# Top-k attention into a hardswish feed-forward: quarter-array products for the left-over queries, and another order of the first loads and transposes

## The chip, the core and the metric

The kernel runs on one core of a Trainium2 chip. A core has five engines with their own instruction streams: TensorE (PE, with its weight loads PEld), VectorE (DVE), ScalarE (ACT), GpSimd (POOL) and SyncE (SP). Each engine executes its instructions in the order of its stream and waits for others by semaphores. Sixteen DMA engines move data between HBM and the on-chip memory SBUF; a DMA is issued by an instruction in an engine's stream. TensorE writes its products into PSUM, which has eight banks; a bank holds 512 float32 in each of 128 partitions.

The metric is the device time of one execution in microseconds, as the median of the runs. Lower is better.

## The reference

Two blocks stand one behind the other. The first is attention over 8 batches, 8 heads, 576 positions and a head size of 64, in which each query attends to its 32 best keys alone. The second is a feed-forward block with hardswish over the 4608 rows of 512 that come out.

```python
scores = scale * np.matmul(q, k.transpose(0, 1, 3, 2))          # (8, 8, 576, 576)
kth = np.partition(scores, -32, axis=-1)[..., -32:-31]
scores = np.where(scores >= kth, scores, -1000000000.0)
scores = scores - np.max(scores, axis=-1, keepdims=True)
attn = np.exp(scores)
attn = attn / (np.sum(attn, axis=-1, keepdims=True) + 1e-09)
x = np.matmul(attn, v)                                           # heads joined: (4608, 512)
h = x @ w_in                                                     # (512, 2048), float64 on input
g = h * np.clip(h + 3.0, 0.0, 6.0) / 6.0
out = g @ w_out                                                  # (2048, 512), float64 on input
```

## The kernel before

**Tiles.** The 576 positions of a head are cut into 4 tiles of 128 (J = 4, JP = 512) and a rest of 64 (R). Two heads make a `Pair`: their keys and queries of 64 values each lie side by side, so that 128 rows hold two heads. A `Duo` is two pairs (four heads) with one tile of queries. There are 64 duos with 128 queries and 16 with the 64 left-over queries (`self.rest`), 80 in all.

**One duo.** `scores` (line 200) multiplies the queries with the keys. Each head takes half the rows of TensorE's array (the slices `heads`); the 512 main keys of a head go to one PSUM bank (line 232, for left-over queries line 215), the 64 left-over keys of both heads to the fifth bank (lines 226 and 217). ScalarE copies the banks into the SBUF tile `sc` (lines 233 and 236; 219 and 220 for left-over queries). `top` (line 243) finds the 32 greatest of each row on VectorE: four rounds of MAX8 (line 250, eight greatest values) with MATCH_REPLACE8 (line 254, which strikes them out) between. `shift`, `exp` and `inverse` (lines 259 to 287) turn the rest into weights: GpSimd takes the difference of the 32nd and the first value, ScalarE runs two activations for each row and sums up, VectorE takes the reciprocal. `weights` (line 289) scales on GpSimd and splits the words into halves, `flip` transposes them by a DMA, `join` (line 314) puts them together on ScalarE or GpSimd, and `values` (line 326) multiplies with the values on TensorE.

**The feed-forward block** (line 352) is a generator of pieces for TensorE (lines 365 and 385), ScalarE (373, 375, 395) and GpSimd (379, 380). `piece` issues one after another between the steps of the attention.

**PSUM.** The pool `ps_big` has one buffer of five banks, which the transposes and the scores take in turn through `big()`: the next user waits until ScalarE has copied the last one out. The pool `ps_w` has three buffers of one bank each for the values and the feed-forward block.

**Weights.** The weights come as float64. `convert` (line 96) makes float32 of them in four steps: SP loads a chunk (line 102); ScalarE takes an absolute value and a scaled copy (108, 111) with a clamp by GpSimd between (109); VectorE shifts and joins bits (117, 118); GpSimd adds (123). There are 32 chunks. Each call of `convert_step` moves the pipeline by one: the add of one chunk, VectorE's two instructions of the next, ScalarE's of a later one, and the load of a further one. VectorE's part of a chunk comes two calls after its ScalarE part.

**Order.** The schedule is written out by hand; every engine's stream has the order of the program. Lines 515 to 527 are the prologue: loads of the first pairs, the transpose of pair 0, its scores, the transpose of pair 1, its scores, with three calls of `convert_step` between. Then come slots (line 564), eight for each duo. A slot has one round of `top`, one `convert_step`, and whatever of the other parts is due (the dictionaries `usual`, `behind`, `early` and `soon`). In the first slots the third and the fourth pair are transposed. After the last duo the pieces of the feed-forward block that are left run out.

**A pair's load** (line 146) has six DMAs on SP: the keys of the first head, of the second, the left-over keys of both, and the same for the queries. `transpose` (line 171) turns nine 128x128 tiles through TensorE into the five banks: tiles 0 to 3 are keys, 4 to 7 queries, and tile 8 has the left-over keys and queries. ScalarE copies them out: 1024 columns (line 179), the left-over queries (180), and the left-over keys of each head into `kr` (183), which has zeros elsewhere.

Of the kernel before, what the change touches and what calls it, by code (L numbers as in the profile page):

```python
# [10 lines left out]
F32 = mybir.dt.float32  # L11
# [18 lines left out]
def kernel(  # L30
# [22 lines left out]
    def pool(name, bufs, **kw):  # L53
        return ctx.enter_context(tc.tile_pool(name=name, bufs=bufs, **kw))
# [23 lines left out]
    w_out = const([P, NFC, DM], "w_out")  # L78
# [9 lines left out]
    def big():  # L88

        return ps_big.tile([P, 5 * 512], F32, tag="big", name="big")  # L90
# [48 lines left out]
    class Pair:  # L139
# [3 lines left out]
            self.b, self.hp = b, hp  # L143
            self.vm, self.vr, self.kr = vms[hp], vrs[hp], krs[b % 2 * NHP + hp]

        def load(self):
            h0 = 2 * self.hp
            t = self.landed = kqpool.tile([P, 2 * J + 1, 2, D], F32, tag="kq", name="landed")
            for i, src in enumerate((k, q)):
                for hh in range(2):  # L150
                    nc.sync.dma_start(
                        t[:, i * J : (i + 1) * J, hh, :],
                        src[self.b, h0 + hh, 0:JP, :].rearrange("(p j) d -> p j d", j=J),
                    )
                nc.sync.dma_start(
                    t[i * R : (i + 1) * R, 2 * J, :, :],
                    src[self.b, h0 : h0 + 2, JP:S, :].rearrange("h s d -> s h d"),
                )
# [9 lines left out]
                    self.vr[hh * R : (hh + 1) * R, hh, :], v[self.b, h0 + hh, JP:S, :]  # L168
                )

        def transpose(self):
            kq = kqpool.tile([P, JP + S], F32, tag="kq", name="kq")
            self.kT, self.qT = kq[:, 0:JP], kq[:, JP : JP + S]
            ps = big()
            for j in range(2 * J + 1):
                rows = self.landed[:, j, :, :].rearrange("p h d -> p (h d)")
                nc.tensor.transpose(ps[:, j * P : (j + 1) * P], rows, ident[:])  # L177
            c0 = 2 * JP
            nc.scalar.copy(kq[:, 0:c0], ps[:, 0:c0])
            nc.scalar.copy(kq[:, c0 : c0 + R], ps[:, c0 + R : c0 + 2 * R])  # L180
            for hh in range(2):
                d = slice(hh * D, (hh + 1) * D)
                nc.scalar.copy(self.kr[d, hh, :], ps[d, c0 : c0 + R])

    class Duo:

# [13 lines left out]
        def scores(self, us=(0, 1)):  # L200

            if us[0] == 0:
                self.sc = scpool.tile([P, 2, 2 * (S + R)], F32, tag="sc", name="sc")
                self.den = mpool.tile([P, 2, 2], F32, tag="den", name="den")
            sc, nu = self.sc[:, us[0] : us[-1] + 1, :], len(us)
            ps = big()
            heads = [slice(0, D), slice(D, P)]
            qs = slice(self.qt * P, min(self.qt * P + P, S))
            banks = ps[:, 0 : 4 * 512].rearrange("p (n s) -> p n s", s=512)
            left = ps[:, 4 * 512 :]  # L210
            if self.rest:
# [8 lines left out]
                nc.scalar.copy(  # L220
                    sc[:, :, JP:S], left[:, 0 : nu * R].rearrange("p (u r) -> p u r", r=R)
                )
                return
            for i, u in enumerate(us):
                pr = self.pairs[u]
                nc.tensor.matmul(
                    left[:, i * P : (i + 1) * P], pr.qT[:, qs], pr.kr[:].rearrange("p h r -> p (h r)")
                )
            for i, u in enumerate(us):
                pr = self.pairs[u]  # L230
                for hh, d in enumerate(heads):
                    nc.tensor.matmul(banks[:, 2 * i + hh, :], pr.qT[d, qs], pr.kT[d, :])  # L232
            nc.scalar.copy(  # L233
                sc.rearrange("p u (h s) -> p (u h) s", h=2)[:, :, 0:JP], banks[:, 0 : 2 * nu, :]
            )
            nc.scalar.copy(  # L236
                sc[:, :, JP : JP + P], left[:, 0 : nu * P].rearrange("p (u r) -> p u r", r=P)
            )

        def row(self, u, t):  # L240
            return self.sc[:, u, t * S : (t + 1) * S]
# [174 lines left out]
    per_batch = 2 * J + 2  # L416
    ND = len(duos)
# [4 lines left out]
    left = 0  # L422
# [123 lines left out]
    queued = {}  # L546
    for m in range(ND):
        for part, at in (early if m < 2 else soon if m >= ND - 2 else behind if per_batch <= m < ND - 4 else usual).items():
            queued.setdefault(8 * m + at, []).append((m, part))

    def parts(slot, late=None):
# [12 lines left out]
    for m in range(ND + 3):  # L564
        u = duos[m] if m < ND else None
        for i in range(8):
# [18 lines left out]
            if i == 0:  # L585
                p = pair_at(m, 4)
# [5 lines left out]
            if i == 5:  # L592
                p = pair_at(m, 5)
# [42 lines left out]
```

## Time and profile before

| what | us |
|---|---|
| median of 3 runs (lowest, highest) | 1580.66 (1580.39, 1581.92) |
| the profiled execution's own time | 1580.33 |
| its span, first instruction to last | 1578.5 |
| first MAX8 starts (line 250) | 13.59 |
| last MAX8 ends | 1491.31 |
| MAX8, all: line 250, `m<-wk` and `m<-sc` | 613.1 + 203.3 busy |
| MATCH_REPLACE8, all: line 254, `wk<-m,wk` and `wk<-m,sc` | 423.7 + 211.8 busy |
| conversion on VectorE: lines 117 and 118, 32 of each | 24.8 + 30.2 busy |
| products of left-over queries: lines 215 and 217, 128 of each | 32.8 + 9.0 busy |

Times in the profile are counted from the start of the span. A line of the timeline gives the start, the length, the engine, the program line, the operation with output and input, the number of instructions merged, and in brackets the idle time of the engine before it with what ended that. A line of the waits gives who waited for whom, the total, the number of waits and the longest. One written matmul of float32 stands in the trace as two MATMUL records.

### The profile page before, as it was taken

The numbers are of one execution on the slowest core, as the hardware profiler recorded it, in microseconds if no ns is written. First come the engines' busy times: TensorE is split into PE (matmuls) and PEld (weight loads), VectorE is DVE, ScalarE is ACT, GpSimd is POOL, SyncE is SP. The second block draws the span as 40 slices with busy tenths as digits, with TensorE's granted clock in tenths as the row PEclk, the third lists the DMA queues.
The fourth block names the chain that finished last, engine by engine and source line by source line (L and its number), as shares of the span: only waits on it lengthen the run. The fifth ranks groups of instructions, "written<-read, shape, count | busy, mean of one in ns | idle before, by whom it ended". The sixth has DMA issues, their size and how long they took to land.

```text
span 1578.5 us, 28787 instructions
## 1 busy us (share of the span) xinstructions
PE 1456.9 (92%) x10272; PEld 1039.0 (66%) x10272; DVE 1466.8 (93%) x3105; ACT 1096.3 (69%) x1865; POOL 1144.5 (73%) x1264
## 2 busy tenths in 40 slices
PE   5256799979999999998999999999999999999899
PEld 3153566567767777666777777776777767677675
DVE  6999999999999999999999999999999999999700
ACT  6675777777777777777776786777766787777621
POOL 4868687777867777867687777867687777767841
PEclk9568999989999999999999999999999999999999
DMA  8652543444344543545254543446244443533410
GB/s 236 159 181 45 113 83 81 94 91 97 76 90 89 101 83 76 101 85 119 55 106 76 97 89 82 93 93 116 57 96 87 98 88 74 103 65 68 83 22 14
DMA packets 450319, 144.49 MB, mean 92 GB/s; under 512 B 433280, under 2 KB 441472, under 8 KB 450176
## 3 DMA queue, kind: packets, MB, share of 16 engines
q1 hardware_dynamic: 450176, 142.65, 43.5%
q8 instruction: 81, 1.33, 0.3%
q14 instruction: 62, 0.51, 0.1%
HBM read 45.09 MB, written 9.44 MB: 35 GB/s over the span
## 4 chain that ended last, share of the span: by engine, by line
DVE 51%; PE 35%; POOL 5%; issue 3%; ACT 3%; DMA 1%; SPq 1%; POOLq 0%; ACTq 0%; DVEq 0%
DVE m L250 26%; DVE wk L254 22%; PE h L365 14%; PE acc L385 13%; PE pv L338 4%; PE big L232 3%; POOL e L306 1%; DVE y L118 1%; POOL sc L297 1%; DMA t<-e 1%; POOL eT L318 1%; DVE a L117 1%; PE big L177 1%; ACT sc L278 1%; ACT eT L318 1%
## 5 line engine op out<-in xcount | busy, mean ns | idle before, releaser
L250 DVE MAX8 m<-wk 128x8 f32<-128x576 f32 x864 | 613.1, 746 | 2.2
L385 PE MATMUL acc<-w_out,g 128*128 128x512 f32 x1152 | 516.9, 600 | 14.1 <-POOL g L380 14.1
L365 PE MATMUL h<-xT,w_in 128*128 128x128 f32 x4096 | 485.5, 279 | 17.3 <-ACT xT L348 17.3
L365 PEld LDWEIGHTS h<-xT,w_in 128*128 128x128 f32 x4096 | 475.0, 195 | 39.5 <-issue 18.2
L254 DVE MATCH_REPLACE8 wk<-m,wk 128x576 f32<-128x576 f32 x576 | 423.7, 742 | 0.0
L385 PEld LDWEIGHTS acc<-w_out,g 128*128 128x128 f32 x1152 | 213.6, 191 | 260.4 <-issue 238.6
L297 POOL TENSOR_SCALAR sc<-sc,den 128x576 f32<-128x576 f32 x288 | 213.8, 753 | 229.9 <-DVE den L287 222.7
L306 POOL COPY e<-sc 128x2304 uint16<-128x2304 uint16 (+1 forms) x192 | 320.3, 1678 | 10.2
L278 ACT ACTIVATE sc<-sc,shift 128x576 f32<-128x576 f32 x288 | 220.4, 769 | 40.5 <-POOL shift L266 37.7
L318 ACT COPY eT<-t 128x2304 uint16<-128x2304 uint16 (+1 forms) x82 | 215.9, 2632 | 37.9 <-DMA t<-e 35.3
L273 ACT ACTIVATE sc<-sc,m 128x576 f32<-128x576 f32 x288 | 210.1, 777 | 46.2 <-DVE m L250 46.0
L338 PE MATMUL pv<-eT,vm 128*64 128x128 f32 (+1 forms) x2560 | 164.0, 273 | 57.9 <-ACT eT L318 45.8
L254 DVE MATCH_REPLACE8 wk<-m,sc 128x576 f32<-128x576 f32 x288 | 211.8, 742 | 0.0
L318 POOL COPY eT<-t 128x2304 uint16<-128x2304 uint16 (+1 forms) x78 | 203.8, 2613 | 6.9 <-DMA t<-e 6.5
L338 PEld LDWEIGHTS pv<-eT,vm 128*64 128x64 f32 x2560 | 135.2, 141 | 109.3 <-ACT eT L318 49.7
L250 DVE MAX8 m<-sc 128x8 f32<-128x576 f32 x288 | 203.3, 742 | 2.4 <-ACT sc L236 2.4
L373 ACT ACTIVATE g<-h,three 128x512 f32<-128x512 f32 x144 | 98.5, 684 | 150.0 <-PE h L365 140.6
L380 POOL TENSOR_TENSOR g<-g,hs 128x512 f32<-128x512 f32 x144 | 185.0, 1285 | 12.1 <-POOL g L379 0.2
L233 ACT COPY sc<-big 128x2048 f32<-128x2048 f32 (+1 forms) x65 | 119.3, 1836 | 26.1 <-PE big L232 26.0
L232 PE MATMUL big<-kq 64*128 64x512 f32 x512 | 136.4, 653 | 0.0
L379 POOL TENSOR_SCALAR g<-g 128x512 f32<-128x512 f32 x144 | 89.2, 620 | 62.6 <-ACT g L373 52.4
L395 ACT ACTIVATE o<-acc 128x512 f32<-128x512 f32 x36 | 21.4, 595 | 106.6 <-PE acc L385 106.6
(47 smaller groups left out, 1113.1 us busy)
## 6 DMA issues: line engine op xcount, KB each, us to landing
landed<-in_k_dram SPq DMA_DIRECT2D x64, 128.0 KB, 3.0
landed<-in_q_dram SPq DMA_DIRECT2D x64, 128.0 KB, 3.0
st<-in_moe_w_in_dram SPq DMA_DIRECT2D x16, 512.0 KB, 5.1
vm<-in_v_dram SPq DMA_DIRECT2D x64, 128.0 KB, 2.3
st<-in_moe_w_out_dram SPq DMA_DIRECT2D x16, 512.0 KB, 6.6
out_dram<-o SPq DMA_DIRECT2D x32, 256.0 KB, 2.4
t<-e SPq DMA_TRANSPOSE x160, 4.6
landed<-in_k_dram SPq DMA_DIRECT2D x32, 32.0 KB, 2.8
```

What stands on the lines that cost most here:

```text
L232: nc.tensor.matmul(banks[:, 2 * i + hh, :], pr.qT[d, qs], pr.kT[d, :])
L250: nc.vector.max(self.m[u][:, t, 8 * r : 8 * r + 8], self.cur[t])
L254: nc.vector.match_replace(wk, self.m[u][:, t, 8 * r : 8 * r + 8], self.cur[t], LOWEST)
L273: nc.scalar.activation(row, row, AF.Prelu, bias=m[:, t, TOP_K - 1 : TOP_K], scale=-1.0, alpha=FLAT)
L278: nc.scalar.activation(row, row, AF.Exp, bias=self.less[u][:, t : t + 1], scale=-scale / FLAT, accum_out=self.den[:, u, t : t + 1],)
L297: nc.gpsimd.tensor_scalar(row, row, self.den[:, u, t : t + 1], 1.0, ALU.mult, ALU.mult)
L306: nc.gpsimd.tensor_copy(halves[:, :, to : to + c1 - c0], words)
L318: copy(eT[:, 0 : self.nb, :] .rearrange("p c q -> p (c q)") .bitcast(U16) .rearrange("p (x h) -> p h x", h=2), self.t16[u][:, 0 : 2 * self ...
L338: nc.tensor.matmul(pv[hh * D : (hh + 1) * D, u * w : (u + 1) * w], pr.vm[:, hh, c, :] if c < J else pr.vr[:, hh, :], rhs, start=(c == 0), ...
L365: nc.tensor.matmul(h[:, (f - f0) * P : (f - f0 + 1) * P], w_in[:, i, f * P : (f + 1) * P], xT[:, i, :], start=(i == 0), stop=(i == NHP - 1),)
L380: nc.gpsimd.tensor_tensor(g[:], g[:], hs[:], ALU.mult)
L385: nc.tensor.matmul(acc[:], gs[f // nf][:, f % nf * P : (f % nf + 1) * P], w_out[:, f, :], start=(f == 0), stop=(f == NFC - 1),)
```

## The change

It has four parts.

*Left-over queries.* In `scores` the product of pair `u` and head `hh` goes to the output half `heads[u ^ hh]` in place of `heads[hh]`. With the row half of the head, the four products of a duo then lie in four different quarters of the array. The four main products are issued first, then the four left-over ones, which go to banks 2 and 3. `values` reads the transposed weights at the columns that go with it.

*The first pair's loads.* `load` takes a queue. For the first pair the three query loads are issued by ScalarE.

*The first pair's transpose.* It uses three banks of `ps_w` in place of `big()`: the key tiles; the first query tile with the left-over tile; the other query tiles. ScalarE copies the first two banks as far as the first scores need them, and the remaining queries later, after the first scores. For those first scores the copies into `sc` are split in three: left-over columns, first bank, second bank.

*The prologue.* VectorE fills one chunk of `w_out` with zeros and TensorE multiplies it with itself twice, ahead of everything else. The conversion step between the first transpose and the first scores is taken out, so that two are left before the slots, both after the first scores; the transpose of the second pair comes before the second of them.

```diff
-        def load(self):
+        def load(self, queue=None):
...
-            for i, src in enumerate((k, q)):
+            for i, (src, eng) in enumerate(((k, nc.sync), (q, queue or nc.sync))):
...
-        def transpose(self):
+        def transpose(self, first=False):
...
+            if first:
+                ps = [ps_w.tile([P, 512], F32, tag="w", name="kqp") for _ in range(3)]
+                turn(ps[0], range(J))
+                turn(ps[1], [J, 2 * J])
+                turn(ps[2], range(J + 1, 2 * J))
+                nc.scalar.copy(self.kT, ps[0][:])
+                nc.scalar.copy(kq[:, JP : JP + P], ps[1][:, 0:P])
+                copy_left(ps[1][:, P:])
+                self.later = [
+                    (kq[:, JP + P : c0], ps[2][:, 0 : JP - P]),
+                    (kq[:, c0 : c0 + R], ps[1][:, P + R : 2 * P]),
+                ]
+                return
...
-                for i, u in enumerate(us):
-                    pr = self.pairs[u]
-                    for d in heads:
-                        nc.tensor.matmul(banks[d, i, :], pr.qT[d, qs], pr.kT[d, :])
-                    for hh, d in enumerate(heads):
-                        nc.tensor.matmul(left[d, i * R : (i + 1) * R], pr.qT[d, qs], pr.kr[d, hh, :])
+                quarters = [
+                    (i, hh, d, heads[u ^ hh])
+                    for i, u in enumerate(us)
+                    for hh, d in enumerate(heads)
+                ]
+                for i, hh, d, to in quarters:
+                    pr = self.pairs[us[i]]
+                    nc.tensor.matmul(banks[to, i, :], pr.qT[d, qs], pr.kT[d, :])
+                for i, hh, d, to in quarters:
+                    pr = self.pairs[us[i]]
+                    nc.tensor.matmul(banks[to, 2 + i, 0:R], pr.qT[d, qs], pr.kr[d, hh, :])
...
+            if us == (0,):
+                (to, src), rest = copies
+                copies = [rest, (to[:, 0, :], src[:, 0, :]), (to[:, 1, :], src[:, 1, :])]
+            for copy in copies:
+                nc.scalar.copy(*copy)
...
-                            rhs = eT[:, c if c < J else J + hh, hh * R : (hh + 1) * R]
+                            rhs = eT[:, c if c < J else J + hh, (u ^ hh) * R :][:, 0:R]
...
-    first[0].load()
+    nc.vector.memset(w_out[:, 0, :], 0.0)
+    ps = big()
+    for _ in range(2):
+        nc.tensor.matmul(ps[:, 0:DM], w_out[:, 0, 0:P], w_out[:, 0, :])
+    first[0].load(nc.scalar)
     land(2)
     first[1].load()
-    first[0].transpose()
-    convert_step()
+    first[0].transpose(first=True)
     duos[0].scores((0,))
+    for copy in first[0].later:
+        nc.scalar.copy(*copy)
     convert_step()
     first[2].load()
+    first[1].transpose()
     convert_step()
-    first[1].transpose()
     duos[0].scores((1,))
     land()
```

More of the change, by code (lines that the diff above doesn't have):

```diff
@@ L144, in __init__ @@
             self.vm, self.vr, self.kr = vms[hp], vrs[hp], krs[b % 2 * NHP + hp]
-        def load(self):
+        def load(self, queue=None):
             h0 = 2 * self.hp
             t = self.landed = kqpool.tile([P, 2 * J + 1, 2, D], F32, tag="kq", name="landed")
-            for i, src in enumerate((k, q)):
+            for i, (src, eng) in enumerate(((k, nc.sync), (q, queue or nc.sync))):
                 for hh in range(2):
-                    nc.sync.dma_start(
+                    eng.dma_start(
                         t[:, i * J : (i + 1) * J, hh, :],
@@ L154, in load @@
                     )
-                nc.sync.dma_start(
+                eng.dma_start(
                     t[i * R : (i + 1) * R, 2 * J, :, :],
@@ L169, in load_values, with turn, copy_left @@
                 )
-        def transpose(self):
+        def transpose(self, first=False):
             kq = kqpool.tile([P, JP + S], F32, tag="kq", name="kq")
             self.kT, self.qT = kq[:, 0:JP], kq[:, JP : JP + S]
+            c0 = 2 * JP
+            def turn(ps, tiles):
+                for i, j in enumerate(tiles):
+                    rows = self.landed[:, j, :, :].rearrange("p h d -> p (h d)")
+                    nc.tensor.transpose(ps[:, i * P : (i + 1) * P], rows, ident[:])
+            def copy_left(ps):
+                for hh in range(2):
+                    d = slice(hh * D, (hh + 1) * D)
+                    nc.scalar.copy(self.kr[d, hh, :], ps[d, 0:R])
+            if first:
[11 more added lines that the diff above has]
+                return
             ps = big()
[L175 to L178, printed above, removed]
+            turn(ps, range(2 * J + 1))
             nc.scalar.copy(kq[:, 0:c0], ps[:, 0:c0])
             nc.scalar.copy(kq[:, c0 : c0 + R], ps[:, c0 + R : c0 + 2 * R])
-            for hh in range(2):
-                d = slice(hh * D, (hh + 1) * D)
-                nc.scalar.copy(self.kr[d, hh, :], ps[d, c0 : c0 + R])
+            copy_left(ps[:, c0:])
     class Duo:
@@ L211, in scores @@
             if self.rest:
-                for i, u in enumerate(us):
-                    pr = self.pairs[u]
-                    for d in heads:
-                        nc.tensor.matmul(banks[d, i, :], pr.qT[d, qs], pr.kT[d, :])
-                    for hh, d in enumerate(heads):
-                        nc.tensor.matmul(left[d, i * R : (i + 1) * R], pr.qT[d, qs], pr.kr[d, hh, :])
+                quarters = [
[9 more added lines that the diff above has]
+                    nc.tensor.matmul(banks[to, 2 + i, 0:R], pr.qT[d, qs], pr.kr[d, hh, :])
                 nc.gpsimd.memset(sc[:, :, S : S + R], 0.0)
                 nc.scalar.copy(sc[:, :, 0:JP], banks[:, 0:nu, :])
-                nc.scalar.copy(
-                    sc[:, :, JP:S], left[:, 0 : nu * R].rearrange("p (u r) -> p u r", r=R)
-                )
+                nc.scalar.copy(sc[:, :, JP:S], banks[:, 2 : 2 + nu, 0:R])
                 return
@@ L232, in scores @@
                     nc.tensor.matmul(banks[:, 2 * i + hh, :], pr.qT[d, qs], pr.kT[d, :])
[L233 to L238, printed above, removed]
+            copies = [
+                (sc.rearrange("p u (h s) -> p (u h) s", h=2)[:, :, 0:JP], banks[:, 0 : 2 * nu, :]),
+                (sc[:, :, JP : JP + P], left[:, 0 : nu * P].rearrange("p (u r) -> p u r", r=P)),
+            ]
+            if us == (0,):
[3 more added lines that the diff above has]
+                nc.scalar.copy(*copy)
         def row(self, u, t):
@@ L547 @@
     for m in range(ND):
-        for part, at in (early if m < 2 else soon if m >= ND - 2 else behind if per_batch <= m < ND - 4 else usual).items():
+        if m < 2:
+            when = early
+        elif m >= ND - 2:
+            when = soon
+        else:
+            when = behind if per_batch <= m < ND - 4 else usual
+        for part, at in when.items():
             queued.setdefault(8 * m + at, []).append((m, part))
```

## The prediction

> **What bounds the kernel now.** I read the busy table and the chain of waits first, then VectorE's waits, then the busy time in three stretches, and last the first 17 us and the stretch where VectorE has its longest wait, instruction by instruction.
>
> ```profile
> PE 1456.9 (92%) x10272; PEld 1039.0 (66%) x10272; DVE 1466.8 (93%) x3105; ACT 1096.3 (69%) x1865; POOL 1144.5 (73%) x1264
> ...
> DVE 51%; PE 35%; POOL 5%; issue 3%; ACT 3%; DMA 1%; SPq 1%; POOLq 0%; ACTq 0%; DVEq 0%
> ```
>
> TensorE and VectorE look like equal bounds. The stretches decide (their cut points are the start of the first MAX8 and the end of the last):
>
> ```profile
> 0.00:13.59 13.59, 5.17 (x15) 2.66 (x15) 1.09 (x4) 5.15 (x10) 3.06 (x19) 1.00 0.76 183
> 13.59:1491.31 1477.72, 1372.73 (x9813) 981.40 (x9813) 1465.51 (x3101) 1071.84 (x1824) 1109.75 (x1215) 0.96 0.46 95
> 1491.31:1578.50 87.19, 79.01 (x445) 54.92 (x444) 0.17 (x1) 19.30 (x33) 31.67 (x31) 0.98 0.10 23
> ```
>
> The columns are length, then PE, PEld, DVE, ACT and POOL busy, clock, DMA share and GB/s. Between its first and last MAX8, VectorE is busy 1465.51 of 1477.72 us: only 12.2 us idle, TensorE 105. So the span is a head of 13.6, VectorE's own work, and a tail of 87.2. The chain's 35% of PE is work that finished just in time. VectorE's waits:
>
> ```profile
> DVE a L117 <- POOL a L109: 13.3, 2, 10.0
> DVE den L287 <- ACT den L283: 9.3, 4, 6.7
> DVE m L250 <- ACT sc L236: 2.4, 2, 1.7
> ```
>
> 10.0 and 1.7 of these lie in the head, 6.7 in the tail. In the body remain 3.3 before a weight conversion at 136.98, some 2.6 before reciprocals and 0.7 before a MAX8: 6.6. The head:
>
> ```profile
> 2.82 1.28 SPq L151 DMA_DIRECT2D landed<-in_q_dram  x2
> 4.14 0.63 SPq L155 DMA_DIRECT2D landed<-in_q_dram  x1
> ...
> 8.01 1.01 ACT L179 COPY kq<-big 128x1024 f32<-128x1024 f32 x1 [6.01 <-PE big L177]
> ...
> 9.55 0.77 PE L226 MATMUL big<-kr,kq 128*128 128x128 f32 x2 [1.58 <-ACT kr L183]
> 10.25 2.08 PE L232 MATMUL big<-kq 64*128 64x512 f32 x4
> 10.87 0.43 DVE L117 TENSOR_SCALAR a<-a 128x512 uint32<-128x512 uint32 x1 [10.02 <-POOL a L109]
> 11.21 0.69 DVE L118 SCALAR_TENSOR_TENSOR y<-st,y 128x512 uint32<-128x512 uint32 x1
> 12.37 1.01 ACT L233 COPY sc<-big 128x1024 f32<-128x1024 f32 x1 [1.68 <-PE big L232]
> 13.59 1.42 DVE L250 MAX8 m<-sc 128x8 f32<-128x576 f32 x2 [1.69 <-ACT sc L236]
> ```
>
> It is serial: load, transpose, copy, scores, copy. TensorE is at half clock, though the clock column, which has no event before 35, says 1.00: nine transposes take 2.18 us at 13.61 and 1.15 at 191.35.
>
> **Quarter products.** A left-over pair of heads takes 2.10 us of TensorE (205.90 to 208.00). That is two groups of about 1.0, one after the other; in each, two half-array products already run side by side. If the four quarters run together, one group is left: about -1.05 for each of 16 such duos, -16.8 of TensorE; if they don't, 0. The eviction copies keep their sizes (1.01 and 0.28). VectorE's 1465.5 us hide the gain, so I take 0. If that cover were gone, all 16.8 would count.
>
> **Head.** Three query loads leave SP (0.65 each, issued 2.82 to 4.77) for ACT, whose string of three would run 0.72 to 2.8 beside SP's keys. The first key transpose starts at 4.54, the first query transpose at 6.64. Two strings share one set of DMA engines (share 0.76), so I put the last query at 5.4 (bounds 4.5 and 6.6). SP's later loads start 1.95 earlier. New on VectorE is a 128x512 fill, with no row like it: 0.4 (as L117) to 0.8 (four times POOL's 128x128 fill of 0.20), in idle time. Then TensorE runs two 128x512 products, which the trace records as two each: eight such records take 3.44 at full clock, so four at half clock take 3.44, from about 1.6 to 5.1. The key transposes queue behind them, 0.5 later than now, but the queries follow without a gap: nine at 0.213 (2.18). The key bank is whole at 6.2, the second bank at 6.6. On ACT the copies of 512, 128 and twice 64 columns (0.58, 0.27, 0.43, each starting 0.1 before the last ends) end at 7.3, where the present ones end at 9.45. From there to the scores' copy the rows give 9.45 to 12.37, 2.9, hence 10.2. The left-over columns are copied meanwhile, and one bank of 512 (0.58) comes before MAX8: 10.8, so **-2.8**. With the clock open by then the products take half: 9.4, -4.2. I take -3.2, near the cold end: at 17.97 TensorE works 2.8 us nearly unbroken, and the nine transposes at 22.05 still take 2.18.
>
> The Trainium skill speaks against the warm-up ("TensorE: Matmul & The Clock Gate", Part 4: PE-mode transpose): transposes don't count as activity that opens the clock. The trace shows only that they run at either clock. By that rule the term is -2.8, without it up to -4.2. On the second queue, the skill ("DMA: Bandwidth & Descriptors", Issuing engines are not separate DMA queues) grants only the time of issue, at most 1.95 for these three.
>
> How much passes on: the fourth pair's transposes start at 25.77, just behind their loads, and VectorE already waits 0.29 for a reciprocal behind them at 32.4. Those loads come 1.95 earlier, plus one weight chunk fewer ahead of them (chunks landed 1.4 apart, at 9.44 and 10.82): 3.35. A larger head gain comes back as a wait there.
>
> **Conversions.** Before, three conversion steps precede the first MAX8, after it two. So the first L117/L118 pair, now free in the head, moves into VectorE's full stretch, and each chunk comes one step later. Moved with it are ACT's two activations, POOL's clamp and add and SP's chunk load. Three things change. In the first step after MAX8 no POOL add runs beside the pair, which then costs about 1.1 and not 2.3 (rows 10.87 and 16.37): -1.2. At the end one more step appears:
>
> ```profile
> 140.45 0.61 POOL L109 TENSOR_SCALAR a<-a 128x512 f32<-128x512 f32 x1 [2.26 <-ACT a L108]
> 141.14 0.61 POOL L379 TENSOR_SCALAR g<-g 128x512 f32<-128x512 f32 x1
> 141.84 2.14 POOL L380 TENSOR_TENSOR g<-g,hs 128x512 f32<-128x512 f32 x1
> 143.93 2.50 POOL L123 TENSOR_TENSOR w_out<-a,y 128x512 int32<-128x512 int32 x2
> ...
> 142.16 0.68 DVE L118 SCALAR_TENSOR_TENSOR y<-st,y 128x512 uint32<-128x512 uint32 x1
> 142.76 1.41 DVE L250 MAX8 m<-wk 128x8 f32<-128x576 f32 x2
> ```
>
> The last chunk's clamp now stands on POOL behind the add at 143.93: 143.93 + 1.25 + 0.61 = 145.8. VectorE is there at 144.1 and waits 1.7, with all later MAX8 queued behind. The pair itself costs 1.0 to 2.4. Sum 1.5 to 2.9; I take **+2.0**. Bounds: -0.3 without the wait, and +5.5 with a wait like that at 136.98 (3.31) and the longest pair (1.7 + 1.7). That older wait stays: the steps around it move as one.
>
> **Tail.** TensorE stands idle 4.41 from 1491.31, then 3.3 us run at clock 0.50 (1496.0 to 1499.3), a loss of 1.7. With less work in front the idle time is longer and half clock likelier, for one or two such windows: -1.7 to +1.7, I take **+0.5**. The rest of the tail is unbroken TensorE work in a fixed order.
>
> **Sum.** -3.2 + 2.0 + 0.5 + 0 = -0.7. The profiled execution (1580.33, span 1578.5 and 1.8 around it) lies 0.33 under the median of 1580.66, so 1579.6 for it and **1580.0** for the median. This case's own range is 1577.5 to 1583.8.
>
> **Rivals.** *Head gain kept* (0.20): the clock opens and the last conversion doesn't wait: -3.4 (the loads' limit) - 0.3 = -3.7, **1577.0**. For it: TensorE is busy for 5.5 us on end, longer than any stretch of the first 30 us now. Against: POOL's order at 143.93.
> *TensorE is the bound* (0.03): all 16.8 count, **1563.9**. For it, the chain's 35%; against, 12.2 idle us of VectorE.
> *Conversions collide* (0.20): the added last step meets POOL's queue as the one at 136.98 does: +5.5, with the head at -2.7 and the tail at +1.0: +3.8, **1584.5**. It decides the sign of the whole once this step costs over 2.7 net, and is measurable over 5.9. For it: L117 and L118 reach 1.7 each beside POOL work.
> *The change doesn't do what it says* (0.06): ACT's table load (1.28 from 0.72) comes before its loads, which then end no earlier than SP's, and the warm-up only delays: head -1.5, total +1.0, **1581.7**.
> The forecast keeps 0.51.
>
> **Numbers.** A measurement here tells some 0.2%, 3.2 us, from no change. Faster is the first two rivals: 0.23. Slower is the third: 0.20. Within: 0.51 + 0.06 = 0.57. The outer bounds of the terms are -5.4 (-3.4 - 0.3 - 1.7) and +5.2 (-2.0 with the queries at 6.6, +5.5, +1.7), 1575.3 to 1585.9; leaving out a tenth on each side gives 1576.5 to 1584.5.
>
> **What would show it.** First MAX8 at 10 to 11; x4 score products of about 2.0 (cold) or 1.0 (open clock); a reciprocal's wait near 30 if the loads limit; a new wait of L117 near 143; left-over duos of about 1.0 on PE with VectorE's body unchanged. I am wrong if VectorE's idle time between first and last MAX8 changes by more than 3 us elsewhere, or if its MAX8 work gets shorter or longer.

## The result, and the profile after

The changed kernel takes 1581.22 us (median of 6 runs, 1580.44 to 1582.04) where the kernel before, run beside it, takes 1581.18 (6 runs, 1580.18 to 1582.21): ratio 1.0, interval 0.9987 to 1.0013. No change that can be measured. But nearly everything inside has moved. The profiled execution has a span of 1579.4, 0.9 more than the 1578.5 of before.

The busy times and the chain of waits of the changed kernel:

```profile
PE 1448.0 (92%) x10276; PEld 1035.6 (66%) x10276; DVE 1468.7 (93%) x3106; ACT 1097.6 (69%) x1868; POOL 1143.0 (72%) x1264
...
DVE 63%; PE 26%; POOL 3%; issue 3%; ACT 2%; SPq 1%; DMA 0%; POOLq 0%; ACTq 0%
```

TensorE lost 8.9 us of work and 9 points of the chain; VectorE gained 1.9 and 12. The stretches, cut again at the start of the first MAX8 and the end of the last (length, then PE, PEld, DVE, ACT, POOL busy, clock, DMA share, GB/s):

```profile
0.00:9.88 9.88, 6.68 (x19) 2.94 (x19) 0.55 (x3) 3.13 (x8) 2.44 (x18) 1.00 0.75 192
9.88:1492.23 1482.35, 1360.71 (x9792) 976.57 (x9793) 1467.98 (x3103) 1075.15 (x1829) 1108.97 (x1216) 0.95 0.46 95
1492.23:1579.40 87.17, 80.59 (x468) 56.13 (x466) 0.17 (x1) 19.27 (x33) 31.63 (x31) 0.98 0.10 23
```

The head is 3.71 shorter (13.59 before), the body 4.63 longer (1477.72), the tail the same. So VectorE starts earlier and ends later. Its waits in the whole execution (us in total, times, longest):

```profile
DVE den L319 <- ACT den L315: 9.2, 2, 6.7
DVE m L282 <- ACT sc L270: 8.5, 1, 8.5
DVE a L117 <- POOL a L109: 6.3, 4, 3.3
```

8.5 is the head and 6.7 the tail. In the body lie one wait for a reciprocal, 2.42, and on L117 the old 3.30 with a new 2.45 and small ones. Before there were four waits on `den`, now two; the two that went, near 419 and 1370, play a part below.

The head, line by line in the timeline (start, duration, engine, line, in brackets the idle time before and what ended it):

```profile
0.72 1.34 ACTq L152 DMA_DIRECT2D landed<-in_q_dram  x2
0.93 0.48 DVE L550 MEMSET w_out<- 128x512 f32 x1
...
1.47 3.78 PE L553 MATMUL big<-w_out 128*128 128x512 f32 x4 [1.47 <-DVE w_out L550]
...
2.77 1.28 ACT L194 ACT_TABLE_LOAD   x1 [2.77 <-issue]
...
5.49 1.38 PE L181 MATMUL kqp<-ident,landed 128*128 128x128 f32 x9 [0.24 <-DMA landed<-in_k_dram]
...
7.92 1.13 PE L261 MATMUL big<-kq 64*128 64x512 f32 x4
8.97 1.73 SPq L156 DMA_DIRECT2D landed<-in_q_dram  x1
9.09 1.24 ACT L270 COPY sc<-big 128x128 f32<-128x128 f32 x3 [1.67 <-PE big L261]
9.88 1.42 DVE L282 MAX8 m<-sc 128x8 f32<-128x576 f32 x2 [8.46 <-ACT sc L270]
...
10.74 0.59 SPq L102 DMA_DIRECT2D st<-in_moe_w_in_dram  x1
```

The nine transposes take 1.38 (2.18 at 13.61 before), the four score products 1.13 and not 2.08: the clock opened near 5.9, after the warm-up and the first transposes. ACT's table load stands behind its DMA issues, not before them. And SP is busy 1.73 us with one small load issue at 8.97, so the next weight chunk goes out at 10.74 (10.85 before).

Where the last conversion now stands, in the timeline of all engines:

```profile
143.31 1.25 POOL L123 TENSOR_TENSOR w_out<-a,y 128x512 int32<-128x512 int32 x1
...
144.60 0.67 ACT L108 ACTIVATE a<-st 128x512 f32<-128x512 f32 x1 [3.25 <-POOL w_out L123]
...
145.35 0.61 POOL L109 TENSOR_SCALAR a<-a 128x512 f32<-128x512 f32 x1 [0.79 <-ACT a L108]
...
146.00 1.49 DVE L117 TENSOR_SCALAR a<-a 128x512 uint32<-128x512 uint32 x1 [2.45 <-POOL a L109]
```

ScalarE's first step of the last chunk waits for the add of the chunk before it, which stands behind two other instructions on POOL; then come ScalarE, the clamp, and VectorE, 2.45 late. The pair that follows is stretched: 1.49 for L117, which took 0.42 in the head.

A left-over duo on TensorE:

```profile
208.74 1.09 PE L245 MATMUL big<-kq 64*64 64x512 f32 x8
209.65 0.29 PE L248 MATMUL big<-kr,kq 64*64 64x64 f32 x8
209.87 1.98 PE L417 MATMUL acc<-w_out,g 128*128 128x512 f32 x4
```

From 208.74 to the next product at 209.87 are 1.13 us, where the duo took 2.10: the four quarters do run together.

The account of the 0.9 us: head -3.71; reciprocal's wait near 30 +2.13 (2.42 against 0.29); two small conversion waits at 16.45 and 20.67, +0.60; new wait at 143.55, +2.45; conversion pairs inside the body 49.14 to 51.62, +2.48; VectorE's waits at 419.43 (0.83), 1369.9 (1.43) and 1373.8 (0.69) gone, -2.95; tail and rest -0.1.

### The profile page after: what moved, and what is told of

Read it like the earlier page. It is cut to its first block, busy times and chain, and to the rows that moved or that the text cites. A ratio compares the mean times of both kernels' runs of the same rounds, so it can differ in the third digit from the quotient of the medians.

```text
span 1579.4 us, 28799 instructions
## 1 busy us (share of the span) xinstructions
PE 1448.0 (92%) x10276; PEld 1035.6 (66%) x10276; DVE 1468.7 (93%) x3106; ACT 1097.6 (69%) x1868; POOL 1143.0 (72%) x1264
## 4 chain that ended last, share of the span: by engine, by line
DVE 63%; PE 26%; POOL 3%; issue 3%; ACT 2%; SPq 1%; DMA 0%; POOLq 0%; ACTq 0%
DVE m L282 33%; DVE wk L286 28%; PE acc L417 10%; PE h L397 10%; PE pv L370 3%; PE big L261 2%; DVE y L118 1%; DVE a L117 1%; POOL e L338 1%; POOL g L412 1%; ACT sc L310 1%; DVE den L319 1%; POOL eT L350 1%; PE big L181 1%; POOL sc L329 1%
## 5 line engine op out<-in xcount | busy, mean ns | idle before, releaser
L417 PE MATMUL acc<-w_out,g 128*128 128x512 f32 x1152 | 521.0, 603 | 16.8 <-POOL g L412 16.8
L270 ACT COPY sc<-big 128x256 f32<-128x256 f32 (+3 forms) x131 | 136.8, 1098 | 17.0 <-PE big L261 16.8
```

The source lines that it names most:

```text
L417: nc.tensor.matmul(acc[:], gs[f // nf][:, f % nf * P : (f % nf + 1) * P], w_out[:, f, :], start=(f == 0), stop=(f == NFC - 1),)
```

## The experiments

The kernels e1 to e12 were timed in five rounds against the kernel before; the row of the changed kernel ("after") is the result above. In the table, "first" is the start of the first MAX8, "body" runs to the end of the last, "waits" are VectorE's idle times of about 0.3 us and more in the body, "pairs" is what L117 and L118 take of VectorE's time there. These four, the tail and the span come from one profiled execution each; runs of one kernel spread over some 2 us, so the ratio is what a verdict rests on, and the columns say where time lies.

| kernel | median (before) | ratio, interval | first | body | waits | pairs | tail | span |
|---|---|---|---|---|---|---|---|---|
| before | | | 13.59 | 1477.72 | 0.29 at 32; 3.31 at 133; three later, 2.95 | 49.14 | 87.2 | 1578.5 |
| after | 1581.22 (1581.18) | 1.0000 [0.9987, 1.0013] | 9.88 | 1482.35 | 0.42; 2.42 at 30; 3.30 at 133; 2.45 at 144 | 51.62 | 87.2 | 1579.4 |
| e1_quarters_only | 1578.06 (1581.48) | 0.9978 [0.9969, 0.9987] | 13.38 | 1474.54 | 0.31; 3.31 | 49.03 | 87.2 | 1575.1 |
| e2_head_only | 1584.05 (1581.48) | 1.0019 [1.0011, 1.0028] | 10.35 | 1485.44 | 2.74; 3.30; 2.45; five later, 4.10 | 50.75 | 88.0 | 1583.7 |
| e3_pair3_sooner | 1579.60 (1581.48) | 0.9988 [0.9979, 0.9996] | 9.91 | 1479.71 | 0.57; 3.30; 2.44 | 51.45 | 88.4 | 1578.0 |
| e4_step_in_slot2 | 1576.05 (1581.48) | 0.9965 [0.9951, 0.9979] | 11.71 | 1476.12 | 3.30 | 50.98 | 88.6 | 1576.5 |
| e5_no_warmup | 1580.68 (1581.15) | 0.9997 [0.9988, 1.0005] | 11.08 | 1479.74 | 1.43; 3.30; 2.44 | 50.66 | 88.5 | 1579.3 |
| e6_queries_on_sp | 1582.13 (1581.15) | 1.0004 [0.9995, 1.0013] | 10.10 | 1481.90 | 0.68; 1.78; 3.30; 2.45 | 51.59 | 87.2 | 1579.2 |
| e7_three_steps | 1576.49 (1581.15) | 0.9966 [0.9952, 0.9979] | 11.51 | 1476.07 | 1.94; 3.30 | 48.92 | 88.2 | 1575.8 |
| e8_steps_2_21_23 | 1573.27 (1581.57) | 0.9947 [0.9934, 0.9961] | 9.98 | 1472.90 | none | 50.86 | 88.6 | 1571.5 |
| e9_both | 1573.32 (1581.57) | 0.9949 [0.9937, 0.9962] | 9.94 | 1473.03 | none | 50.85 | 88.5 | 1571.5 |
| e10_quarters_steps | 1573.06 (1581.57) | 0.9950 [0.9937, 0.9962] | 13.58 | 1470.55 | 0.61 | 48.08 | 87.9 | 1572.0 |
| e11_three_steps_more | 1572.11 (1580.70) | 0.9941 [0.9929, 0.9953] | 10.76 | 1470.66 | 1.27 | 47.57 | 87.2 | 1568.6 |
| e12_plain_head | 1572.40 (1580.70) | 0.9946 [0.9932, 0.9959] | 12.07 | 1470.66 | 2.01 | 46.83 | 88.0 | 1570.8 |

### The two halves of the change apart: e1 and e2

e1 is the kernel before with the quarter products alone (the `quarters` lists, the copy from banks 2 and 3, the new columns in `values`).

> The kernel before with the quarter-array products alone. In the changed kernel the 16 left-over duos end within 1.20 us on TensorE instead of 2.10, and VectorE's waits at 419 (0.83), 1370 (1.43) and 1374 (0.69) are gone. Theory A (the quarter products took those waits away): they vanish here too, VectorE's idle time between first and last MAX8 falls from 12.2 to about 9.3, time 2 to 3 us below before. Theory B (they went because the earlier start shifted the phases of POOL and ACT): the three waits stand, time as before within 1 us. Theory C (TensorE is the bound): 16 x 0.9 = 14 us below before.

e2 is the kernel after with the old left-over products:

```diff
-                    (i, hh, d, heads[u ^ hh])
...
-                    nc.tensor.matmul(banks[to, 2 + i, 0:R], pr.qT[d, qs], pr.kr[d, hh, :])
+                    for d in heads:
+                        nc.tensor.matmul(banks[d, i, :], pr.qT[d, qs], pr.kT[d, :])
+                    for hh, d in enumerate(heads):
+                        nc.tensor.matmul(left[d, i * R : (i + 1) * R], pr.qT[d, qs], pr.kr[d, hh, :])
```

> The changed kernel with the left-over products as they were before. First MAX8 at 9.9 as in the changed kernel, the waits of VectorE at 29.7 (2.4) and 143.6 (2.5) stay. Theory A (the quarter products took the waits at 419 and 1370 away): they come back, time 2 to 3 us above the changed kernel, so 1 to 4 us above before. Theory B (phase shift by the head): they stay away, time as the changed kernel, within 1 us.

e1 takes 0.9978 [0.9969, 0.9987] of the time before, e2 1.0019 [1.0011, 1.0028]. So the result "no change" is a gain of some 3.4 us and a loss of some 2.6, and theory A holds in both: the waits of 1.43 and 0.69 near 1370 are gone in e1 and stand again in e2 (1.41 and 0.69), the one of 0.83 near 419 comes back as 0.46. VectorE's waits in e1, then the two of e2 that matter:

```profile
DVE a L117 <- POOL a L109: 13.2, 2, 9.9
DVE den L290 <- ACT den L286: 7.0, 2, 6.7
DVE m L253 <- ACT sc L239: 1.6, 1, 1.6
```

```profile
DVE den L316 <- ACT den L312: 12.9, 6, 6.7
...
DVE m L279 <- POOL eT L347: 0.7, 1, 0.7
```

In e1 the waits for `den` fall from 9.3 in four to 7.0 in two; in e2 they are six. Two of the six stand where the kernel before had none (0.91 at 1184 and 0.63 at 1274), so the shift by the head is not without effect either. How does a TensorE that is off VectorE's path reach it? The timeline of all engines, before:

```profile
404.17 3.70 PE L385 MATMUL acc<-w_out,g 128*128 128x512 f32 x8
...
404.30 2.10 POOL L306 COPY e<-sc 128x2304 uint16<-128x2304 uint16 x1
...
407.91 0.60 ACT L395 ACTIVATE o<-acc 128x512 f32<-128x512 f32 x1 [3.25 <-PE acc L385]
...
408.54 0.35 SPq L397 DMA_DIRECT2D out_dram<-o  x1
...
409.00 2.79 SPq L312 DMA_TRANSPOSE t<-e  x1
```

The same place in e1:

```profile
401.99 3.70 PE L388 MATMUL acc<-w_out,g 128*128 128x512 f32 x8
...
404.04 2.10 POOL L309 COPY e<-sc 128x2304 uint16<-128x2304 uint16 x1
405.72 0.60 ACT L398 ACTIVATE o<-acc 128x512 f32<-128x512 f32 x1 [2.50 <-PE acc L388]
...
406.35 0.35 SPq L400 DMA_DIRECT2D out_dram<-o  x1
...
406.81 2.97 SPq L315 DMA_TRANSPOSE t<-e  x1
```

The transpose of the weights has its input at 406.4 (404.30 + 2.10), but SP issues in order, and ahead of it stands the store of `o`, which waits for TensorE's accumulation. So the transpose starts 2.6 late, at 409.00; ScalarE's `join` behind it starts at 414.34, where e1's starts at 412.18, and ScalarE then is late with the sums that the reciprocal needs at 419. In e1 TensorE is 2.2 us ahead, the store leaves at 406.35, and the wait doesn't arise. Near 1362 it is value loads (L163), waiting for TensorE's `pv`, that stand ahead of a transpose. This chain is read off the timelines; no run moves the store or these loads alone.

### The wait near 30: e3

```diff
+            if m == 0 and i == 0:
+                first[3].load()
             convert_step()
-            if m == 0 and i == 0:
-                first[3].load()
```

> The changed kernel with the loads of the fourth pair issued ahead of one weight chunk instead of behind it. Theory A (VectorE's wait of 2.42 at 29.66 is set by the landing of the fourth pair's loads, 26.1): they land 1.3 sooner, at about 24.8, TensorE's nine transposes end 1.2 to 1.4 sooner, the wait falls to 1.0 to 1.2, time 1.2 us below the changed kernel. Theory B (the wait is set by TensorE at half clock and ScalarE's copies in a row, not by loads): wait and time stay.

In the changed kernel the fourth pair's transposes wait for the loads, and the reciprocal comes behind them:

```profile
25.09 2.25 PE L181 MATMUL big<-ident,landed 128*128 128x128 f32 x9 [3.31 <-DMA landed<-in_k_dram]
```

```profile
32.08 0.17 DVE L319 RECIPROCAL den<-den 128x2 f32<-128x2 f32 x1 [2.42 <-ACT den L315]
```

In e3 the fourth pair's last load landed at 23.2, against 26.1 in the changed kernel, and the reciprocal's wait fell from 2.42 to this:

```profile
29.59 0.17 DVE L319 RECIPROCAL den<-den 128x2 f32<-128x2 f32 x1 [0.57 <-ACT den L315]
```

So it was these loads, as theory A has it. In this run the weight chunks too landed about 1 us sooner (8.2 and 9.8), so not all of the 2.9 is the edit's. Time: 0.9988 [0.9979, 0.9996], an interval that overlaps that of the changed kernel.

The other runs say the same more sharply. The reciprocal starts 6.02 us after the fourth pair's last load in the kernel before (26.66 and 32.68), 5.99 after it in the changed kernel (26.09 and 32.08), and 5.98 to 6.04 in e1, e2, e5 to e8 and e10 to e12, whose first MAX8 lie between 9.98 and 13.58. Only in e3, where the transposes wait for ScalarE's copies and no longer for a load, is it 6.40, and in e4 and e9 VectorE doesn't wait there. So as long as VectorE waits for this reciprocal, the loads set it and the first MAX8 doesn't: of the 3.71 us that the new head is shorter, 0.60 are left at this point (32.68 to 32.08).

### The wait near 144: e4 and e7

e4 puts a third conversion step back, in slot 2:

```diff
+            if m == 0 and i == 2:
+                convert_step()
             if m == 0 and i in (1, 2):
```

> The changed kernel with one more conversion step in slot 2, ahead of the fourth pair's transposes there are left to do. All later chunks are one slot earlier, so the last conversion falls where it did before. Theory A (the step that the change put off costs 2.45 of wait at 143.6 and 2.5 of VectorE's work, and one VectorE pair more in front of the reciprocal at 29.7 is free, since VectorE waits 2.42 there): the wait at 143.6 is gone, the one at 29.7 falls to about 1.4, time 4 to 5 us below the changed kernel (about 1576.5). Theory B (the cost of the put-off step is only its own pair, and the wait at 143.6 moves elsewhere): 1 us below or less.

e7 puts it back where it was, ahead of the first scores:

```diff
     first[0].transpose(first=True)
+    convert_step()
     duos[0].scores((0,))
```

> The changed kernel with the conversion step between the first transpose and the first scores put back. ScalarE then waits for the first weight chunk (landed 9.3) ahead of the copies of the first scores: first MAX8 at 11.3 to 11.5, 1.5 later. Theory A (the put-off step costs 4.9): the wait at 143.6 and the extra pair in VectorE's body are gone, the wait at 29.7 stays near 2.4 because one more chunk is loaded ahead of the fourth pair; time 3 to 3.5 us below the changed kernel. Theory B (the put-off step costs little): 1.5 us above the changed kernel.

Both take away the wait at 143.55, and both are faster by a like amount: 0.9965 [0.9951, 0.9979] and 0.9966 [0.9952, 0.9979]. That is theory A, by somewhat more than it gave: beside the kernel before that was run with each, e4's median is 5.4 and e7's 4.7 lower, where the changed kernel's is level. In e4 the first MAX8 of the profiled execution comes 1.8 us later than in the changed kernel, because its keys landed and its clock opened later (see the end). In e4 of VectorE's waits only the first and one of 3.3 remain on these lines:

```profile
DVE m L282 <- ACT sc L270: 10.3, 1, 10.3
DVE a L117 <- POOL a L109: 3.3, 1, 3.3
```

In e7 the first pair again runs in front of the first MAX8, while VectorE has nothing else to do:

```profile
10.57 0.43 DVE L117 TENSOR_SCALAR a<-a 128x512 uint32<-128x512 uint32 x1 [9.15 <-POOL a L109]
...
11.51 1.41 DVE L282 MAX8 m<-sc 128x8 f32<-128x576 f32 x2
```

It gives 1.63 us of the head back (11.51 against 9.88) and gains 6.28 in the body: 2.45 of the wait, 2.70 of the pairs (51.62 to 48.92), the rest of smaller waits. The 1.63 cost nothing further on: the reciprocal near 30 starts at 32.11 here and at 32.08 in the changed kernel. So the order of the prologue cost more than the earlier start brought.

### The parts of the head: e5 and e6

e5 leaves out the warm-up (the fill, its bank and the two products):

```diff
-    nc.vector.memset(w_out[:, 0, :], 0.0)
-    ps = big()
-    for _ in range(2):
-        nc.tensor.matmul(ps[:, 0:DM], w_out[:, 0, 0:P], w_out[:, 0, :])
```

> The changed kernel without VectorE's fill and the two products ahead of the first transposes. In the changed kernel the clock opened at about 5.9 us and the score products of the first pair took 1.1 us against 2.1. Theory A (the warm-up brings the clock, but its gain is lost where the fourth pair's loads limit): key transposes still start near 5.4, as the loads allow, first MAX8 at 11.2 to 11.4 (1.4 later), VectorE's wait at 29.7 falls from 2.4 to 1.0 to 1.2, time the same as the changed kernel within 0.5 us. Theory B (the warm-up matters to the end): time 1.4 us above the changed kernel. Theory C (it only delays the transposes): first MAX8 at 9.9 or sooner.

e6 leaves the queries on SP:

```diff
-    first[0].load(nc.scalar)
+    first[0].load()
```

> The changed kernel with the first pair's queries back on SP's queue. Theory A (the second queue brings the first queries about 1 us sooner, and nothing for later loads, since SP is held up behind the weight chunks in either case): last query lands near 6.7 against 5.6, first MAX8 at about 11, the weight chunks and the fourth pair land within 0.6 us of the changed kernel's times (26.1), VectorE's wait at 29.7 falls by about the 1 us that MAX8 starts later, time within 0.7 us of the changed kernel. Theory B (the head start of SP's later loads matters): the fourth pair lands 1.9 later, time 1.9 us or more above the changed kernel.

Without the warm-up the first MAX8 comes 1.2 later, and the time is the same (0.9997 [0.9988, 1.0005]): theory A. The reciprocal's wait is 0.99 shorter, but that isn't the later MAX8 alone: in this execution the fourth pair's last load landed at 24.83, 1.26 sooner than in the changed kernel, and the reciprocal started 1.26 sooner (30.82). The tail is 1.2 longer. What the warm-up gains at the start ends at a reciprocal that waits for the loads.

With the queries on SP the first MAX8 comes at 10.10, only 0.2 later, where about 11 was expected: a miss. The queries do land later (6.6 against 5.55), but the keys land sooner (4.9 against 5.77), and the keys come first. The fourth pair's last load lands at 25.9, no later than with the second queue (26.1), and SP issues the chunk behind the second pair's loads at 10.72, where it was 10.74: SP's head start doesn't reach them, as theory A said. Time 1.0004 [0.9995, 1.0013].

### Without the waits: e8 and e9

```diff
+            if 8 * m + i in (2, 21, 23):
+                convert_step()
```

> The kernel with the added step in slot 2, and two more steps, in slots 21 and 23, so that the last conversion falls in slot 28, ahead of the slot in which every kernel so far has VectorE waiting 3.3 near 133. Theory A (that wait belongs to the conversions of the last slots, which stand behind ScalarE's feed-forward copy and GpSimd's queue): it vanishes, no new one, time about 3.3 below the kernel with the step in slot 2, so near 1572.8. Theory B (the wait belongs to GpSimd's backlog there, whatever the conversions do): VectorE waits about as long elsewhere between 95 and 150, time the same within 1 us.

e9 is e8 with e3's edit.

> As the kernel with steps in slots 2, 21 and 23, and the fourth pair's loads one weight chunk sooner. Theory A (the loads still limit the reciprocal near 29.7 when the first MAX8 is as early as 9.9): a wait of up to 1.4 there becomes 0.3 or less, time 0.5 to 1 us lower. Theory B (ScalarE then waits for the chunk that now lands 1.3 later, in the same chain): no change within 0.5 us.

e8 takes 0.9947 [0.9934, 0.9961]: slot 2 as in e4, and the two extra steps move the conversions away from the POOL order behind the old wait of 3.3, which is gone as well, as A had it. The body in its window:

```profile
9.98:1482.88 1472.90, 1360.10 (x9792) 976.20 (x9793) 1467.11 (x3103) 1075.92 (x1829) 1109.30 (x1216) 0.95 0.47 95
```

VectorE is busy 1467.11 of 1472.90. The wait near 30 is 0.14 here, so e9 finds nothing left to gain, 0.9949 [0.9937, 0.9962]: theory B by the time, though not by its reason. The step in slot 2 gives VectorE other work before that reciprocal (a sixth conversion pair, at 22.73); in e9 the last load lands 1.8 sooner (23.84 against 25.64), and the reciprocal starts at 31.84 without any wait, against 31.68 in e8.

### What the head is worth: e10, e11, e12

e10 is e1 with e8's edit in slots 21 and 23 only; it has nothing of the new head.

```diff
+            if 8 * m + i in (21, 23):
+                convert_step()
```

> The kernel before with the quarter products and two more steps in slots 21 and 23, none of the head's changes. If the wait near 133 belongs to the last conversions it vanishes here too, 3.3 below the quarter products alone, near 1574.8. Its distance to the kernel with the head and three added steps is what the head is worth: Theory A, 1.5 to 2 us (first MAX8 2 to 3.5 sooner, less what the loads take back); Theory B, nothing.

e11 is the kernel after with the edits of e3, e7 and e10; e12 is e11 without the warm-up and with the queries on SP.

> The changed kernel with the third conversion step put back ahead of the first scores, two more steps in slots 21 and 23, and the fourth pair's loads one weight chunk sooner. Theory A (what the head gains goes back into VectorE's body as the moved conversion pair, 2.8 us; with the step put back the first pair runs in the head again): first MAX8 at 11.5, body as in the quarter products with two more steps (1470.5), wait near 30 under 1, time 1 to 2 us below 1573.06, near 1571.5. Theory B (a head gain never passes): time 1573 within 0.5.

> The same without the warm-up products and with the first queries on SP's queue. Theory A (the first conversion waits for the first weight chunk at 9.3, so warm-up and second queue are hidden behind it): first MAX8 at 11.5 to 12, time within 0.5 us of the kernel with them. Theory B (they set the first MAX8 here too): 1 to 2 us later and slower.

The bodies of e10 and of e11:

```profile
13.58:1484.14 1470.56, 1359.61 (x9813) 975.72 (x9813) 1464.33 (x3101) 1072.98 (x1824) 1108.33 (x1215) 0.97 0.46 95
```

```profile
10.76:1481.41 1470.65, 1358.55 (x9792) 974.09 (x9793) 1463.76 (x3102) 1074.43 (x1827) 1109.53 (x1215) 0.96 0.47 95
```

e10 starts 3.6 later than e8 (13.58 against 9.98) and is as fast (0.9950 [0.9937, 0.9962]). That is nearer to theory B, but intervals of 2 us to each side don't exclude the 1.5 of theory A. VectorE's busy time in the body is 2.8 less, 1464.33 against 1467.11, as the first pair lies in front of it; 0.7 is the tail's. With that step put back, e11 has the lowest ratio of all, 0.9941 [0.9929, 0.9953], and its body is that of e10 to 0.1, so its earlier first MAX8 shows in its span (1568.6 against 1572.0). But the medians lie 8.6 (e11) and 8.5 (e10) below the kernel before run beside each, and the intervals overlap. Whether the new head is worth anything at all beside the other two edits stays open. e12, with neither warm-up nor second queue, lies within 0.3 us of e11's median, as A had it. But its reason, that both are hidden behind the first weight chunk, doesn't hold: the first MAX8 comes 1.31 later (12.07 against 10.76), the fourth pair's last load lands 1.27 later, and the profiled span is 2.1 longer. So these two parts bring nothing that the intervals show; B's lower end of 1 us isn't excluded.

## Why the prediction was right, and where its steps were not

The forecast, no change with VectorE as the bound, was right, and 1580.0 lies 1.2 under the measured median. But it is right as a sum; four terms are off and cancel, and that they cancel is luck. The sum was -0.7 for the profiled execution, +0.9 was measured in its span.

- *First MAX8, -3.2 ("near the cold end"; bounds -2.8 and -4.2):* measured -3.71. The mechanism is as worked out, with the warm-up's records from 1.47 to 5.25 (predicted 1.6 to 5.1); only the choice near the cold end was a little off, since the clock opened among the transposes.
- *"How much passes on ... 3.35. A larger head gain comes back as a wait there":* the place is right, the limit is not. 2.42 us of wait came there, 2.13 more than before, with a head gain hardly over the limit. "Those loads come 1.95 earlier, plus one weight chunk fewer" is the step that failed. The last of them landed at 26.09 against 26.66, only 0.57 sooner, and the reciprocal came 0.60 sooner. Of the 1.95, SP had 0.11 left at the chunk behind the second pair's loads (issued at 10.74 against 10.85): the issue ahead of that chunk took 1.73 from 8.97 to 10.70. Before, the same issue took 1.39 and ended at 10.80, as a weight chunk landed (10.82); in e6 it ended at 10.68, with a chunk at 10.70; in the changed kernel the chunk landed at 10.99. So SP's issue seems to stand until an earlier load is through, and three loads issued elsewhere free SP of an issue time that it then spends waiting; e6 shows it, where the three are back on SP and the chunk leaves at 10.72. The chunk fewer did bring the third pair's last load in 1.57 sooner (17.67 against 19.24), but the next chunk landed only 0.58 sooner (20.76 against 21.34). Where that lead went, no run shows.
- *Conversions, +2.0 (bounds -0.3 and +5.5):* measured +4.93 by the wait and the pairs. The new wait came where and how it was said, 2.45 at 143.55 for 1.7 "near 143"; the chain to it has one step more, as ScalarE's activation also waits for the add at 143.31. The term that failed is "-1.2": the pair beside no POOL add did get shorter (0.42 and 0.69 at 12.66), but the stretch turned up in other pairs (1.49 and 1.09 at 20.85), so that the pairs together cost 2.48 and not -0.2 to 1.2. With that, the third rival (+5.5 for this term) had the size of this step nearly right; it ends elsewhere because of the next one.
- *Quarter products, 0: "VectorE's 1465.5 us hide the gain":* the 1.05 per duo is right (2.10 to 1.13), the 0 is wrong: -2.95 of waits went, and e1 shows 0.9978 [0.9969, 0.9987] for it alone. The working itself listed "some 2.6 before reciprocals" and "0.7 before a MAX8" in the body and did not follow them back. Two of them lead over ScalarE, a DMA transpose and SP's order to TensorE. It is neither "all 16.8" nor nothing: it is the waits whose chain passes TensorE. These 2.95 stay just under the prediction's own sign of being wrong, 3 us of VectorE's idle time elsewhere.
- *Old wait at 136.98 stays:* it does, 3.30; only e8 to e12 take it away.
- *Tail, +0.5 (bounds -1.7 and +1.7):* 87.17 against 87.19. Other runs of the study had 87.2 to 88.6, up to 1.4 more, so the range was used.

Head -0.5, loads +2.7 (with the small conversion waits), conversions +2.9, quarter products -2.95, tail -0.5 against their terms: that makes the +1.6 between -0.7 and +0.9 to the rounding.

## What to carry to other kernels

Where one engine is full, an earlier start is worth no more than the next input comes earlier, less what the work that it displaces costs: here 0.60 of 3.7 us of head were left at the first reciprocal that waits for loads, and one conversion pair (2.5 to 2.8) that used to run for free in the head, with the later wait that a pipeline one step behind brings (2.45), took more than that. Every idle microsecond of the full engine has to be followed back to its end, through in-order DMA queues too: a store that waits for TensorE held up the transposes behind it, and 0.97 us per duo off an engine with 100 us to spare became 3 us. Two lines that add a conversion step in slots 21 and 23 showed a gain (e1 0.9978, e10 0.9950, intervals apart); the redesigned head showed none that the intervals can tell.

## What the runs showed of the hardware

**The clock's opening varies with the same warm-up.** With the same head, the clock opened near 5.9 in the changed kernel (transposes 1.38) and only near 10.4 in e4, whose keys landed later:

```profile
1.47 3.78 PE L553 MATMUL big<-w_out 128*128 128x512 f32 x4 [1.47 <-DVE w_out L550]
6.13 2.15 PE L181 MATMUL kqp<-ident,landed 128*128 128x128 f32 x9 [0.88 <-DMA landed<-in_k_dram]
...
9.12 1.75 PE L261 MATMUL big<-kq 64*128 64x512 f32 x4
```

With 0.88 us of idle time in place of 0.24 all nine transposes ran at half clock, and the first MAX8 came at 11.71 and not 9.88. The gap alone didn't do it, for in e11 the transposes are fast behind one of 0.81:

```profile
6.06 1.38 PE L181 MATMUL kqp<-ident,landed 128*128 128x128 f32 x9 [0.81 <-DMA landed<-in_k_dram]
```

The other seven kernels with the same warm-up, the changed one among them, opened between 4.8 and 6.8 by the profile's clock. Why e4's stayed shut until 10.4 is not settled; e4's profiled execution (1578.26) lies 2.2 above its median, so others of its executions may have opened sooner. Without any warm-up (e5) the clock opened near 9.65, that is 1.7 us after the first ordinary product (7.94) and 4.0 after the first transpose (5.60). The Trainium skill ("TensorE: Matmul & The Clock Gate", Part 1: The HAM clock gate) has a free-running window of about 3.4 us that must be busy, which fits the scatter of these openings. Its Part 4 (PE-mode transpose) says that transposes don't count as such work; with that, and if the whole window must be busy, e5 could not have opened before 11.3, an estimate from the page's 3.4 and the run's 7.94. The measurement decides: here the transposes seem to have counted.

**A second queue moves the loads, it doesn't speed them up.** Against e6, ScalarE's queue brought the first pair's queries 1.0 us sooner (5.55 against 6.59) and its keys 0.8 later (5.77 against 4.94). That agrees with the Trainium skill ("DMA: Bandwidth & Descriptors", Issuing engines are not separate DMA queues), by which only the time of issue is saved; here even that came to 0.2 us at the first MAX8.

**The stretch of a VectorE instruction beside POOL work moves on.** L117 takes 0.42 alone and up to 1.49, L118 0.68 and up to 1.09 in the rows named here; taking one POOL neighbour away moved the stretch to other pairs. POOL work alone isn't enough for it: at 141.21 L117 took 0.41 beside POOL's product of line 412.
